# Wider V matmuls and one chunk of K in each of three units moved from DVE to PE in a two-layer decode kernel

## Chip, cores and metric

The kernel runs on one core of one Trainium2 chip. The metric is device time in microseconds (us) of one execution. The engines are named as the profile names them: PE (TensorE matmuls; PEld are its weight loads), DVE (VectorE), ACT (ScalarE), SP (SyncE, which issues the loads here). "Clock" is the share of full clock that the chip grants the PE array; the records show only 0.5 and 1.0 (129 periods of each in the trace before), and means of the two.

## What is computed

Two layers, each an attention block and a small MLP, for two batch entries and one query token. Cut to what matters:

```python
B, Sq, D = 2, 1, 576
H, Sk, Dh = 32, 16384, 128

def _A_ref(x, k_cache, v_cache, wq, wo):          # attention over a cache
    q = (x @ wq).reshape(B, Sq, H, Dh).transpose(0, 2, 1, 3)
    scores = einsum("bhqd,bhkd->bhqk", q, k_cache) * (Dh ** -0.5)
    p = softmax(scores)
    o = einsum("bhqk,bhkd->bhqd", p, v_cache)
    return o.transpose(0, 2, 1, 3).reshape(B, Sq, H * Dh) @ wo
# x = x + A(layernorm(x)); x = x + MLP(layernorm(x)); and both once more, with the same caches
```

There are 64 "units" (batch entry times head) per layer. One unit reads 4.19 MB of K and 4.19 MB of V, in bf16. Both layers together read 1096 MB, and each element of K and V that is read meets one multiplication per layer: this is a kernel of loads.

## The kernel before

SBUF has three places for a unit's K and V. Loads are queued as soon as the place is free; one layer keeps two units for the next. K arrives with a position per row, so a score needs either a transpose on PE, a copy out of PSUM on ACT and a matmul with one column (`turn`, `score`), or a multiplication and a sum on DVE (`dots`). A unit's 128 K blocks are 16 chunks of 8; `ncp` says how many chunks go to PE and ACT, the rest goes to DVE.

```python
def ncp(self, l, i):                              # chunks of unit i on PE; NCH is 16
    return self.NCH // 2 + (3, 2)[min(i, 1)] if l == 1 and i < 2 else self.NCH // 2 + 1

def turn(self, l, i, c):
    ...                                           # 8 transposes of 128x128 per chunk
            ins = pe.transpose(self.tps[b][:, j * 128:(j + 1) * 128],
                               kt[:, (j0 + j) * 128:(j0 + j + 1) * 128], self.ident[:, :])
    ...                                           # then ACT copies tps to ktsb
def score(self):
    ...                                           # 8 matmuls of ONE column
            ins = pe.matmul(self.sps[sp][:, col:col + 1], lhsT=self.ktsb[k][:, j, :],
                            rhs=self.qcur[:, sp:sp + 1], start=True, stop=True)
def weigh(self, l, i, h):                         # V work: 64 matmuls of ONE column per half
    ...
            ins = pe.matmul(self.ops[q][:, 0:1], lhsT=vt[:, j * 128:(j + 1) * 128],
                            rhs=self.p[q][:, h * self.TB + j:h * self.TB + j + 1], ...)
    ...
def attention(self, l):
    ...
    first = (2, self.ROT)[l]                      # ROT = 8: where the hardware loop starts
    self.s.loops.append((l * U + first, (U - first) // 2, 2, ...))
    for i in range(U):
        early = l == 1 and 1 <= i < first
        ...                                       # turn, score, dots of unit i, interleaved
                if early and c == 4:
                    self.weigh(l, i - 1, 0); self.weigh(l, i - 1, 1)
        ...
        if now: self.weigh(l, i - 1, 0)           # otherwise V work comes at the unit's END
        while self.waiting: self.score()
        if now: self.weigh(l, i - 1, 1)
```

Most units run in a hardware loop, two units to a turn, but units 0 and 1 of layer 1, units 0 to 7 of layer 2 and all of the MLPs are written out as straight-line code. And V work is the last PE work of a looped unit, while in the early units of layer 2 it sits in the middle, before the remaining transposes.

## Time and profile before

| | before |
|---|---|
| time, median of 3 runs | 2564.07 us (2563.78 to 2564.38) |
| bytes, mean rate | 1096.38 MB, 428 GB/s |
| load queue, share of 16 DMA engines | 99.7% |
| PE, DVE, ACT busy | 65%, 68%, 48% |
| mean granted PE clock | 0.674 |

The page of the profiled execution. The first line is the busy time of the engines; the next two have 40 columns, one per slice of 64 us (granted clock in tenths; GB/s). Then come the load queue (packets, MB, share of the 16 DMA engines' time), the chain that ended last by engine, and two of the costliest groups, PE's transposes and its V matmuls (busy us, mean ns of one, idle time just before and who ended it).

```profile
PE 1671.5 (65%) x36847; PEld 1559.0 (61%) x36847; DVE 1751.6 (68%) x2595; ACT 1231.3 (48%) x1944; POOL 1.0 (0%) x12
...
PEclk8666666666666666766666666666666666666665
...
GB/s 409 430 431 433 431 430 433 432 431 432 430 433 432 431 432 431 433 431 431 426 408 431 428 432 430 432 433 431 432 432 430 432 431 431 433 432 431 430 433 341
...
q1 hardware_dynamic: 46888, 1095.66, 99.7%
...
DMA 59%; issue 16%; DVE 13%; PE 10%; ACT 1%; SPq 0%; DVEq 0%
...
L798 PE MATMUL tps<-ident,buf 128*128 128x128 bf16 x9240 | 911.7, 263 | 616.5 <-DMA buf<-in_A_k_cache_dram 600.4
...
L870 PE MATMUL ops<-p,buf 128*128 128x1 bf16 x16384 | 461.7, 164 | 66.5 <-DMA buf<-in_A_v_cache_dram 57.4
```

The load queue is busy for 99.7% of the span, and the rate leaves 430 to 433 GB/s in only five slices: the first (409), three around the turn between the layers (426, 408, 428), and the last (341). The PE group of the transposes waited 600 us for K in all. PE's idle time is not the problem; it is the sign that something else sets the pace.

The same core in stretches: start and end, length, busy time of PE, PEld, DVE, ACT and POOL with counts, granted clock, DMA share, GB/s.

```profile
1180.00:1200.00 20.00, 12.69 (x282) 11.60 (x282) 13.74 (x21) 10.01 (x16) 0.00 (x0) 0.67 1.00 433
1280.00:1300.00 20.00, 13.68 (x285) 12.70 (x285) 3.05 (x19) 1.49 (x6) 0.00 (x0) 0.50 1.01 405
1300.00:1320.00 20.00, 16.35 (x323) 15.38 (x321) 7.85 (x19) 6.86 (x11) 0.00 (x0) 0.56 0.95 386
...
1340.00:1360.00 20.00, 16.75 (x341) 15.80 (x337) 16.35 (x26) 13.43 (x23) 0.00 (x0) 0.66 0.98 421
...
1380.00:1400.00 20.00, 18.01 (x355) 17.70 (x353) 18.15 (x27) 13.96 (x20) 0.00 (x0) 0.59 1.00 425
...
2550.00:2560.00 10.00, 9.74 (x143) 8.82 (x144) 0.17 (x1) 0.00 (x0) 0.00 (x0) 0.50 0.17 65
```

One ordinary stretch (1180), then the turn between the layers (1280, 1300), where transfer is lost; the stretches after it move 421 and 425 GB/s again. After about 2554 us there is nothing left to load.

PE's timeline at the end of a looped unit (start, length, operation, count; in brackets the idle time before it and what ended it), then in the third unit of layer 2:

```profile
654.22 0.61 PE L798 MATMUL tps<-ident,buf 128*128 128x128 bf16 x8
...
655.67 1.76 PE L870 MATMUL ops<-p,buf 128*128 128x1 bf16 x64 [0.40 <-DMA buf<-in_A_v_cache_dram]
...
657.69 1.78 PE L870 MATMUL ops<-p,buf 128*128 128x1 bf16 x64
...
666.81 0.50 PE L798 MATMUL tps<-ident,buf 128*128 128x128 bf16 x3 [7.21 <-DMA buf<-in_A_k_cache_dram]
```

```profile
1343.95 3.51 PE L870 MATMUL ops<-p,buf 128*128 128x1 bf16 x128 [0.26 <-ACT p L856]
1347.33 0.91 PE L798 MATMUL tps<-ident,buf 128*128 128x128 bf16 x7
1350.26 0.27 PE L798 MATMUL tps<-ident,buf 128*128 128x128 bf16 x1 [2.02 <-issue]
...
1350.58 1.01 PE L798 MATMUL tps<-ident,buf 128*128 128x128 bf16 x8
```

In the looped unit, transposes take 0.61 us per 8 (full clock), then V work (lines with `ops`) runs 64 matmuls in about 1.8 us, and then PE waits 7.2 us for the next K. In the early unit V work sits before transposes, and after it these take 1.01 us per 8 (half clock).

### The profile page before, as it was taken

What the parts mean: (1) busy time and instruction counts of PE and PEld (TensorE: products, weight loads), DVE (VectorE), ACT (ScalarE), POOL (GpSimd) and SP (SyncE); (2) the same over time, 40 slices, a digit from 0 to 9 for tenths busy, and PEclk for the clock granted to TensorE, in tenths of its full rate; (3) what the DMA queues carried; (4) which work ended last, traced back from release to release, by engine and by line L of the source; (5) the groups of instructions that cost most, each with busy time, mean ns of one, the idle gap of its engine ahead of it and who ended that gap; (6) DMA issues with size and microseconds to landing.
All of it is one profiled execution on the core that took longest, in us unless ns stands there. A gap on an engine that the chain in (4) does not pass through costs nothing.

```text
span 2562.7 us, 84020 instructions
## 1 busy us (share of the span) xinstructions
PE 1671.5 (65%) x36847; PEld 1559.0 (61%) x36847; DVE 1751.6 (68%) x2595; ACT 1231.3 (48%) x1944; POOL 1.0 (0%) x12
## 2 busy tenths in 40 slices
PE   5666666666666656666688766666656666665666
PEld 5555665565565656655678765565656555565566
DVE  5676767677666766766648777666767766676674
ACT  4544544454445445544446554454445544544452
POOL 0000000000000000000000000000000000000000
PEclk8666666666666666766666666666666666666665
DMA  9999999999999999999999999999999999999998
GB/s 409 430 431 433 431 430 433 432 431 432 430 433 432 431 432 431 433 431 431 426 408 431 428 432 430 432 433 431 432 432 430 432 431 431 433 432 431 430 433 341
DMA packets 46936, 1096.38 MB, mean 428 GB/s; under 512 B 4964, under 2 KB 6056, under 8 KB 11560
## 3 DMA queue, kind: packets, MB, share of 16 engines
q1 hardware_dynamic: 46888, 1095.66, 99.7%
q8 instruction: 40, 0.66, 0.1%
q14 instruction: 8, 0.07, 0.0%
HBM read 1095.64 MB, written 0.00 MB: 428 GB/s over the span
## 4 chain that ended last, share of the span: by engine, by line
DMA 59%; issue 16%; DVE 13%; PE 10%; ACT 1%; SPq 0%; DVEq 0%
DMA buf<-in_A_k_cache_dram 56%; DVE prod L827 11%; PE tps L798 6%; DMA buf<-in_B_w_dram 1%; DVE sd L830 1%; PE misc L846 1%; DMA buf<-in_A_v_cache_dram 1%; PE ops L870 1%; ACT ktsb L802 1%; PE misc L693 1%; DMA buf<-in_A_wq_dram 0%; PE sps L815 0%; SPq L435 0%; PE sps L655 0%; ACT p L856 0%
## 5 line engine op out<-in xcount | busy, mean ns | idle before, releaser
L802 ACT ACTIVATE ktsb<-tps 128x1024 bf16<-128x1024 bf16 x1155 | 1124.2, 1031 | 871.2 <-PE tps L798 866.2
L798 PE MATMUL tps<-ident,buf 128*128 128x128 bf16 x9240 | 911.7, 263 | 616.5 <-DMA buf<-in_A_k_cache_dram 600.4
L798 PEld LDWEIGHTS tps<-ident,buf 128*128 128x128 bf16 x9240 | 735.0, 120 | 643.1 <-DMA buf<-in_A_k_cache_dram 619.7
L830 DVE TENSOR_REDUCE sd<-prod 128x8 f32<-128x1024 bf16 x893 | 1089.5, 1220 | 31.0
L827 DVE TENSOR_TENSOR prod<-buf,qb 128x1024 bf16<-128x1024 bf16 x893 | 608.6, 682 | 11.4 <-DMA buf<-in_A_k_cache_dram 10.5
L870 PE MATMUL ops<-p,buf 128*128 128x1 bf16 x16384 | 461.7, 164 | 66.5 <-DMA buf<-in_A_v_cache_dram 57.4
L870 PEld LDWEIGHTS ops<-p,buf 128*128 128x128 bf16 x16384 | 443.7, 100 | 76.4 <-DMA buf<-in_A_v_cache_dram 66.4
L848 DVE TENSOR_REDUCE small<-misc 128x1 f32<-128x128 f32 x128 | 37.3, 292 | 635.8 <-PE misc L846 635.8
L815 PE MATMUL sps<-qcur,ktsb 128*128 128x1 bf16 x9240 | 396.8, 166 | 109.0 <-ACT ktsb L802 88.2
L815 PEld LDWEIGHTS sps<-qcur,ktsb 128*128 128x128 bf16 x9240 | 348.4, 101 | 172.2 <-ACT ktsb L802 166.1
L781 ACT ACTIVATE qb<-misc 128x128 bf16<-128x128 f32 x130 | 36.0, 277 | 369.2 <-PE misc L778 369.2
L846 PE MATMUL misc<-identS,small 128*128 128x128 f32 x256 | 94.4, 472 | 5.2 <-DVE small L840 5.2
L846 PEld LDWEIGHTS misc<-identS,small 128*128 128x128 f32 x256 | 69.7, 332 | 5.8 <-DVE small L840 5.7
L856 ACT ACTIVATE p<-sps,small 128x72 bf16<-128x72 f32 x128 | 41.4, 324 | 6.8 <-DVE small L848 6.8
L856 ACT ACTIVATE p<-sd,small 128x56 bf16<-128x56 f32 x128 | 44.6, 349 | 0.0
L773 ACT ACTIVATE qcur<-qt 128x1 bf16 (+1 forms) x130 | 29.4, 226 | 16.8 <-DVE qt L703 16.8
L778 PE MATMUL misc<-ident,qcur 128*128 128x128 bf16 x130 | 34.6, 266 | 1.3 <-ACT qcur L773 1.3
L925 PE MATMUL misc<-lpiece,small 128*128 128x16 f32 x28 | 8.5, 385 | 41.0 <-DVE lpiece L923 41.0
L925 PEld LDWEIGHTS misc<-lpiece,small 128*128 128x128 f32 x28 | 7.0, 311 | 43.6 <-DVE lpiece L923 43.6
L836 DVE TENSOR_REDUCE small<-sps 128x1 f32<-128x72 f32 x128 | 28.5, 223 | 4.1 <-PE sps L815 4.1
L693 PE MATMUL misc<-prod,buf 128*128 128x2 bf16 (+1 forms) x360 | 24.6, 179 | 6.6 <-DMA buf<-in_B_w_dram 4.6
L693 PEld LDWEIGHTS misc<-prod,buf 128*128 128x128 bf16 (+1 forms) x360 | 22.4, 111 | 8.8 <-issue 4.7
(94 smaller groups left out, 270.8 us busy)
## 6 DMA issues: line engine op xcount, KB each, us to landing
buf<-in_A_k_cache_dram SPq DMA_DIRECT2D x124, 4096.0 KB, 24.3
buf<-in_A_v_cache_dram SPq DMA_DIRECT2D x122, 4096.0 KB, 33.6
buf<-in_A_v_cache_dram SPq DMA_DIRECT2D x5, 2048.0 KB, 22.5
buf<-in_B_w_dram SPq DMA_DIRECT2D x8, 1152.0 KB, 30.7
buf<-in_A_wq_dram SPq DMA_DIRECT2D x8, 1024.0 KB, 9.0
buf<-in_A_wo_dram SPq DMA_DIRECT2D x14, 576.0 KB, 34.6
buf<-in_A_k_cache_dram SPq DMA_DIRECT2D x3, 2048.0 KB, 11.2
buf<-in_A_v_cache_dram SPq DMA_DIRECT2D x4, 1024.0 KB, 23.8
```

Of the source, the lines that this page charges most:

```text
L693: ins = pe.matmul(out[lo:128, t * self.B:(t + 1) * self.B], lhsT=w[:, t * 128:(t + 1) * 128 - lo], rhs=rhs, start=(first and t == 0), stop ...
L778: self.pe(lambda pe: pe.matmul(self.misc[:, 0:128], lhsT=bcast(self.qcur[:, q:q + 1], 128), rhs=self.ident[:, :], start=True, stop=True), ...
L781: self.act(lambda a: a.activation(out=self.qb[q][:, :], in_=self.misc[:, 0:128], func=ACT.Copy), r=["P:misc"], w=[f"qb{q}"])
L798: ins = pe.transpose(self.tps[b][:, j * 128:(j + 1) * 128], kt[:, (j0 + j) * 128:(j0 + j + 1) * 128], self.ident[:, :])
L802: self.act(lambda a: a.activation(out=self.ktsb[k][:, :, :].rearrange("p a b -> p (a b)"), in_=self.tps[b][:, :], func=ACT.Copy), r=[f"P:t ...
L815: ins = pe.matmul(self.sps[sp][:, col:col + 1], lhsT=self.ktsb[k][:, j, :], rhs=self.qcur[:, sp:sp + 1], start=True, stop=True)
L827: self.dve(lambda v: v.tensor_tensor(out=self.prod[d][:, :, :], in0=k3, in1=bcast_mid(self.qb[q][:, :], self.CH), op=ALU.mult), r=[*res, f ...
L830: self.dve(lambda v: v.tensor_reduce(out=self.sd[q][:, o:o + self.CH], in_=self.prod[d][:, :, :], axis=AX.X, op=ALU.add), r=[f"prod{d}"], ...
L846: self.pe(lambda pe: pe.matmul(self.misc[:, 128:256], lhsT=bcast(self.m[:, q:q + 1], 128), rhs=self.identS[:, :], start=True, stop=True), ...
L848: self.dve(lambda v: v.tensor_reduce(out=self.bias[:, q:q + 1], in_=self.misc[:, 128:256], axis=AX.X, op=ALU.max, negate=True), r=["P:misc ...
L856: self.act(lambda a, u, c0=c0, c1=c1, src=src: a.activation(out=self.p[q][:, c0:c1], in_=src, func=ACT.Exp, bias=self.bias[:, q:q + 1], sc ...
L870: ins = pe.matmul(self.ops[q][:, 0:1], lhsT=vt[:, j * 128:(j + 1) * 128], rhs=self.p[q][:, h * self.TB + j:h * self.TB + j + 1], start=(h ...
```

## The change

The intent rests on what the trace before shows: the clock falls while PE does its one-column V work (by the clock records, in 48 of the 49 looped units of layer 1 whose V work lies in 250-1220 us it is 1.0 when the V work begins and 0.5 when it ends). That this is because one column keeps the array busy for too little of the time was my guess; no run had shown it. With 32 equal columns per V matmul (only column 0 is used) the array should be busy for longer, the clock should stay full if the guess is right, and PE should then have room for a tenth chunk in the units early in layer 2, where units run back to back.

```diff
+    WIDE = 32
...
-        return self.NCH // 2 + (3, 2)[min(i, 1)] if l == 1 and i < 2 else self.NCH // 2 + 1
+        return self.NCH // 2 + ((3, 2, 2, 2, 2)[i] if l == 1 and i < 5 else 1)
...
-                    ins = pe.matmul(self.ops[q][:, 0:1], lhsT=vt[:, j * 128:(j + 1) * 128],
-                                    rhs=self.p[q][:, h * self.TB + j:h * self.TB + j + 1],
+                    at = h * self.TB + j
+                    ins = pe.matmul(self.ops[q][:, 0:self.WIDE], lhsT=vt[:, j * 128:(j + 1) * 128],
+                                    rhs=bcast(self.p[q][:, at:at + 1], self.WIDE),
                                     start=(h == 0 and j == 0), stop=(h == 1 and j == self.TB - 1))
```

Unit 1 of layer 2 had 10 chunks before; only units 2, 3 and 4 get one more on PE and one less on DVE.

## The prediction

> **What bounds it now.** The transfers. The queue table gives the one load queue 99.7% of the span on 16 DMA engines: 1096 MB at a mean of 428 GB/s, 430 to 433 in most slices. [...] A unit (8.39 MB of K and V) takes about 19.4 us of transfer, with PE busy 13 us, DVE 14, ACT 10 (table of stretches). In the chain of waits K loads hold 56%; PE waits 600 us in all for K, about 5.8 us per unit.
>
> Transfer time is lost at the start, in the turn between layers (405 GB/s in 1280-1300 us, 386 in 1300-1320), and at the end (no load after about 2554 us, while 180 matmuls of w4 run 12.3 us).
>
> **What the change does.** No load changes.
> 1. V work: 16384 matmuls of one column get 32. They now come every 27.5 ns (64 in 1.75 to 1.85 us) at either clock. In the timeline the clock falls with this work: transposes before it take 0.61 us per 8, after it 1.01. [...] Transposes of 128 columns come every 56 ns at full clock and 107 at half, so 32 columns should stream in 14 and 27 ns (estimate). I expect 27 to 31 ns per V matmul still, and full clock through it.
> 2. Layer 2, units 2 to 4: PE and ACT take 10 chunks, not 9 (unit 1 has 10 already), DVE 6, not 7. A chunk is 1.85 us on DVE, 1.03 on ACT.
>
> **What is on the path.** In a normal unit [...]the first 16 transposes stay at half clock (1.89 us); DVE's seven chunks (13 us) still set the compute. Saved PE time becomes waiting.
> Early in layer 2 (1325 to 1415 us) units run back to back in 14 to 16 us. I expect 12.5 to 13.5, until data is missing. But 1320 to 1480 us already moves 430 GB/s and K loads take up to 35 us from issue to landing, so the queue is full; at most 1 us can be won.
> The loss in the turn comes from w3, gelu, w4, layer norm and wq. Its w4 matmuls take 67 to 68 ns each, as did 25 like them at 37 us at a higher clock; neither turn nor end gains.
>
> **Prediction.** 2563 us, within 2557 to 2569. Faster by 2%: 0.01; within 2%: 0.98; slower: 0.01.
>
> **What would show it.** Span within 0.2%; DMA over 99%, same MB. Mean granted clock up from 0.674 to about 0.80. V matmuls 64 in 1.7 to 2.0 us. PE busy down from 1671 to 1550-1650 us, waits for K up. Layer 2's units 1 to 4 each 1.5 to 3 us shorter, then longer K waits before 1415 us. About 12.3 us of w4 matmuls at the end.
>
> **What would make it wrong.** If 32 columns do not overlap the weight load at half clock, V matmuls cost about 53 ns, 3.3 us more per unit: inside the 5.8 us of slack, but turn and end could lose 1 to 3 us each. If the queue does run dry early in layer 2 (at 1333 us a V load came only just in time), earlier frees win 1 to 3 us.

Its sum stays 2563 us: the span before, less at most 1 us that loads could still win. That loads are near their limit rests on the 99.7% of the queue and the 430 to 433 GB/s of most slices alone, and "full clock through it" was a guess. The trace before has the transposes 55 ns (median) from start to start at full clock and 107 at half, V matmuls 25 and 27, and the clock at 0.76 during the 25 matmuls at 37 us, for 0.50 during those of the end. That weight loads and matmuls overlap shows in PE and PEld busy for 65% and 61% of one span; the 53 ns without overlap are an estimate, 27 ns between V matmuls and 27 of streaming, both at half clock, one after the other.

## The result

The changed kernel took 2563.49 us (median of 4 runs, 2563.30 to 2563.77), the kernel before 2563.93 us in the runs beside it. The ratio is 0.9998, with a 95% interval of 0.9981 to 1.0016: no difference. Ratios here and below are the mean time of one kernel's fast runs over that of the other's in the same rounds, so not quite the ratio of the medians quoted.

The page after, with the lines that answer those of before (the queue's line is the same to the digit, the chain has DMA at 60% for 59%):

```profile
PE 1659.3 (65%) x36895; PEld 1545.7 (60%) x36895; DVE 1746.4 (68%) x2589; ACT 1232.8 (48%) x1947; POOL 1.0 (0%) x12
...
PEclk8767777677667766767768777777677767777676
...
GB/s 409 430 430 433 431 431 433 431 430 433 430 433 431 431 433 431 430 432 432 426 412 428 428 431 434 431 430 433 432 429 432 432 432 431 429 434 432 430 431 347
...
L799 PE MATMUL tps<-ident,buf 128*128 128x128 bf16 x9264 | 902.4, 260 | 619.1 <-DMA buf<-in_A_k_cache_dram 600.4
...
L874 PE MATMUL ops<-p,buf 128*128 128x32 bf16 x16384 | 463.5, 181 | 68.6 <-DMA buf<-in_A_v_cache_dram 58.2
```

The clock row rose here and there (mean 0.674 to 0.723) and nothing else moved: same bytes, same rate slice by slice, same 600.4 us of waiting for K. PE busy fell by only 12 us, far less than I expected. The stretches after the turn:

```profile
1280.00:1300.00 20.00, 13.50 (x288) 12.42 (x288) 3.06 (x19) 1.49 (x6) 0.00 (x0) 0.50 1.02 409
1300.00:1320.00 20.00, 16.26 (x323) 15.14 (x324) 7.99 (x19) 7.00 (x11) 0.00 (x0) 0.58 0.95 384
...
1380.00:1400.00 20.00, 15.00 (x383) 14.41 (x383) 14.90 (x23) 12.60 (x19) 0.00 (x0) 0.91 1.00 428
```

The transfer rates are those of before within a few GB/s, though PE's clock is much higher in the 1380 stretch (0.91 for 0.59). The timelines, first of the same looped unit, then of the third unit of layer 2:

```profile
655.61 1.77 PE L874 MATMUL ops<-p,buf 128*128 128x32 bf16 x64 [0.39 <-DMA buf<-in_A_v_cache_dram]
...
657.62 1.84 PE L874 MATMUL ops<-p,buf 128*128 128x32 bf16 x64
...
666.75 0.50 PE L799 MATMUL tps<-ident,buf 128*128 128x128 bf16 x3 [7.18 <-DMA buf<-in_A_k_cache_dram]
```

```profile
1345.23 3.37 PE L874 MATMUL ops<-p,buf 128*128 128x32 bf16 x128
1348.45 0.55 PE L799 MATMUL tps<-ident,buf 128*128 128x128 bf16 x7
1351.41 0.27 PE L799 MATMUL tps<-ident,buf 128*128 128x128 bf16 x1 [2.42 <-issue]
...
1351.73 1.01 PE L799 MATMUL tps<-ident,buf 128*128 128x128 bf16 x8
```

V work costs what it did: 64 matmuls in 1.77 and 1.84 us, for 1.76 and 1.78. In the looped unit nothing follows it except 7.2 us of waiting, so even a clock held through it would have nothing to speed up. In the early unit it works as intended for 7 transposes (0.55 us for 7, where before they took 0.91), and then an idle time without releaser comes (2.42 us), after which the clock is at half again. These idle times early in layer 2, totals from 1280 to 1500 us, before and then after (us in total, times, longest):

```profile
PE ops L870 <- issue: 4.1, 3, 1.7
...
PE tps L798 <- issue: 2.9, 3, 2.0
...
PE sps L815 <- issue: 1.5, 2, 0.9
```

```profile
PE ops L874 <- issue: 6.8, 4, 2.7
PE sps L816 <- issue: 6.2, 3, 2.4
...
PE tps L799 <- issue: 5.3, 3, 2.4
```

With one gap of 1.8 us in the MLP, the same in both and not shown, that is 4.1 + 2.9 + 1.5 + 1.8 = 10.3 us before, and 6.8 + 6.2 + 5.3 + 1.8 = 20.1 us after. From query matmul to query matmul, units 1 to 4 of layer 2 took 15.0, 15.4, 15.7 and 14.2 us before, and 15.6, 17.2, 15.8 and 15.9 us after. They became longer, not shorter, and the total did not notice.

Taken together, PE spent the 60.3 us of these four units before with 51.3 us of work, 4.8 us of idle time without releaser and 3.9 us of waiting for ACT; after, the 64.4 us were 52.7, 8.5 and 3.0 (the rest are short gaps; worked out from the traces). So PE's work did not shrink: three moved chunks bring 24 transposes and 24 score matmuls, which took what the higher clock gave. Most of the added length is idle time without releaser. These are single executions, though: `tail_pieces` and `unroll24` below, whose code is the same here, showed 16.8 and 10.9 us of such idle time in 1280-1500 us, for 20.1, and took 61.9 and 62.6 us for the four units.

### The profile page after: what moved, and what is told of

Its sections match the earlier page's. It is cut to its first block, busy times and chain, and to the rows that moved or that the text cites. A ratio compares the mean times of both kernels' runs of the same rounds, so it can differ in the third digit from the quotient of the medians.

```text
span 2561.6 us, 84113 instructions
## 1 busy us (share of the span) xinstructions
PE 1659.3 (65%) x36895; PEld 1545.7 (60%) x36895; DVE 1746.4 (68%) x2589; ACT 1232.8 (48%) x1947; POOL 1.0 (0%) x12
## 3 DMA queue, kind: packets, MB, share of 16 engines
q1 hardware_dynamic: 46888, 1095.66, 99.7%
## 4 chain that ended last, share of the span: by engine, by line
DMA 60%; issue 16%; DVE 13%; PE 10%; ACT 1%; SPq 0%; DVEq 0%
DMA buf<-in_A_k_cache_dram 53%; DVE prod L828 11%; PE tps L799 5%; DMA buf<-in_A_v_cache_dram 4%; DMA buf<-in_B_w_dram 3%; DVE sd L831 1%; PE misc L847 1%; PE ops L874 1%; PE misc L694 1%; ACT ktsb L803 1%; PE sps L816 0%; DMA buf<-in_A_wq_dram 0%; SPq L436 0%; DVE small L849 0%; SPq L421 0%
## 5 line engine op out<-in xcount | busy, mean ns | idle before, releaser
L799 PE MATMUL tps<-ident,buf 128*128 128x128 bf16 x9264 | 902.4, 260 | 619.1 <-DMA buf<-in_A_k_cache_dram 600.4
L799 PEld LDWEIGHTS tps<-ident,buf 128*128 128x128 bf16 x9264 | 727.0, 119 | 643.2 <-DMA buf<-in_A_k_cache_dram 617.5
L831 DVE TENSOR_REDUCE sd<-prod 128x8 f32<-128x1024 bf16 x890 | 1085.8, 1220 | 30.8
L874 PE MATMUL ops<-p,buf 128*128 128x32 bf16 x16384 | 463.5, 181 | 68.6 <-DMA buf<-in_A_v_cache_dram 58.2
L857 ACT ACTIVATE p<-sps,small 128x72 bf16<-128x72 f32 (+1 forms) x128 | 41.7, 326 | 6.3 <-DVE small L849 6.3
L857 ACT ACTIVATE p<-sd,small 128x56 bf16<-128x56 f32 (+1 forms) x128 | 44.7, 349 | 0.0
L774 ACT ACTIVATE qcur<-qt 128x1 bf16 (+1 forms) x130 | 29.6, 228 | 16.9 <-DVE qt L704 16.9
L837 DVE TENSOR_REDUCE small<-sps 128x1 f32<-128x72 f32 (+1 forms) x128 | 28.5, 223 | 11.9 <-PE sps L816 11.9
```

The lines of the kernel that those rows point to most:

```text
L799: ins = pe.transpose(self.tps[b][:, j * 128:(j + 1) * 128], kt[:, (j0 + j) * 128:(j0 + j + 1) * 128], self.ident[:, :])
L831: self.dve(lambda v: v.tensor_reduce(out=self.sd[q][:, o:o + self.CH], in_=self.prod[d][:, :, :], axis=AX.X, op=ALU.add), r=[f"prod{d}"], ...
L857: self.act(lambda a, u, c0=c0, c1=c1, src=src: a.activation(out=self.p[q][:, c0:c1], in_=src, func=ACT.Exp, bias=self.bias[:, q:q + 1], sc ...
L874: ins = pe.matmul(self.ops[q][:, 0:self.WIDE], lhsT=vt[:, j * 128:(j + 1) * 128], rhs=bcast(self.p[q][:, at:at + 1], self.WIDE), start=(h ...
```

## The experiments

Four theories. **T**: transfers bind everywhere that counts, so nothing done to PE, ACT or DVE shows. **C**, a rival: the two halves of the change cancel. **G/H**: 32 columns are too few to hold the clock (H), and a held clock would have won time (G). **F**: PE waits for its own instructions wherever code is not looped, which explains the early units. All 12 experiments gave a result; the edits are against the changed kernel unless told otherwise.

### The halves alone

`wide_alone` puts the old `ncp` back; `chunks_alone` has `WIDE = 1`.

> V work 32 columns wide, chunks as before. Theory T (the transfers bind, so nothing on PE, ACT or DVE counts): within 0.15% of before, DMA share over 99%. Rival C (the two parts cancel: the wider V work gains, the moved chunks lose, or the other way round): this run and the run with the chunks alone differ from before by over 0.3% in opposite directions. Profile: granted clock as in the changed kernel, about 0.72.

> 10 chunks on PE in units 1 to 4 of layer 2, V work one column wide. Theory T: within 0.15% of before. Rival C: over 0.3% away, opposite in sign to the run with the wide V work alone. Profile: granted clock as before, about 0.675; units 2 to 4 of layer 2 not shorter than before if PE waits for its instructions there.

Measured: 2563.88 us with the wide V work alone (ratio 0.9998, interval 0.9982 to 1.0015, clock 0.727), 2563.45 us with the chunks alone (0.9999, 0.9982 to 1.0015, clock 0.675). Neither half does anything, so C falls. Both halves act where they should: the first moves the clock, the second does not. With the chunks alone units 2 to 4 took 15.6, 15.6 and 16.0 us, so they are not shorter either; there the idle time without releaser was as before (10.7 us in 1280-1500 us), and it is PE's work that grew, to 53.4 us in units 1 to 4.

### More columns

```diff
-    WIDE = 32
+    WIDE = 64      # wide64;  WIDE = 128 in wide128
```

> As the changed kernel, but 64 columns. At full clock a V matmul comes every 27.5 ns; 32 columns are about 14 ns of array time, half of it, 64 are 27 ns, nearly all of it (estimate from the 56 ns of 128 columns). Theory H (32 columns keep the array busy enough only at half clock): the clock now stays full through the V work, mean granted clock 0.78 to 0.85 instead of 0.72. [...] Time: theory T within 0.15% of before either way; rival G (the gain is missing because the clock was not held) over 0.5% faster than before.

> As the changed kernel, but 128 columns: about 56 ns per V matmul at full clock, so 3.6 us more PE work per unit, about 460 us in all. Theory T: PE has 5.8 us idle per unit, so within 0.3% of before, PE busy up to about 2050 to 2200 us, PE's waits for K down by 350 to 450 us. Rival E (PE's work is on the path): 5 to 18% slower. Clock at or above that of 64 columns.

With 64 columns: 2564.18 us (ratio 1.0003, interval 0.9986 to 1.0019), clock 0.834. That is in the range of H. The clock records, laid over the matmuls of units 10 to 59 of layer 1, show it directly: the share of V matmuls that began at full clock was 0.54 before, 0.56 with 32 columns and 0.89 with 64; of the transposes it was 0.49, 0.54 and 0.54. So in this kernel 32 columns did not hold the clock through V work and 64 mostly did, and the transposes gained nothing by it. That 32 are too few wherever they stand does not follow: in `light_after` below they bring the V matmuls from 0.71 to 1.00. What decides it there, no run isolates. G falls: the clock was the one wanted and nothing was won. The V work of one looped unit in that run:

```profile
911.56 3.46 PE L874 MATMUL ops<-p,buf 128*128 128x64 bf16 x64 [0.71 <-DMA buf<-in_A_v_cache_dram]
...
915.28 2.14 PE L874 MATMUL ops<-p,buf 128*128 128x64 bf16 x64
```

The second half shows what 64 columns cost at full clock, 2.14 us, so 33 ns each and not the 27.5 I had written; the first half began at half clock and took 3.46, 54 ns each.

With 128 columns the clock is 0.907, a V matmul takes 68 ns in the mean over both clocks (1113.7 us over 16384; the 56 expected were a guess from the transposes, for full clock), the transposes take 226 ns each instead of 260 in the mean, PE is busy 2153.9 us, and PE's waits for K fall from 600.4 to 60.7 us. The time is 2578.87 us, ratio 1.0063 (1.0046 to 1.0080). About 500 us of added PE work cost 15 us. The looped units still take the same: 19.61 us in the mean of units 10 to 59 of layer 1, for 19.64 before. So the slack was real: 600.4 us in 105 waits, 5.7 us each, or 4.7 us per unit over all 128. The waits fell by 540 us, more than the 350 to 450 I had expected, and the 15 us are more than the 0.3% that I had allowed T. In stretches:

```profile
1240.00:1260.00 20.00, 17.04 (x287) 15.46 (x285) 14.12 (x21) 9.89 (x17) 0.00 (x0) 0.91 1.00 429
...
1280.00:1300.00 20.00, 12.93 (x285) 12.06 (x284) 3.73 (x23) 1.49 (x6) 0.00 (x0) 0.68 0.77 288
...
1340.00:1360.00 20.00, 18.35 (x327) 17.68 (x325) 12.54 (x18) 10.46 (x16) 0.00 (x0) 0.91 0.88 366
```

An ordinary stretch (1240) moves 429 GB/s with PE busy 17 of 20 us. The loss is in the turn: DMA share 0.77 and 288 GB/s in 1280-1300 us, where before it was 1.01 and 405, and 0.88 in 1340-1360. Counted by bytes delivered, this trace and the one before are level within 0.5 us up to 550 MB and 12 us apart at 700 MB, so most of the loss is there. In the chain that ended last V work has 26%, for 1% before: it is likely on the path to the frees that the next loads wait for, a reading of the trace that no run isolates. So T needs its limit said: nothing shows as long as loads are queued; in the turn, PE can take the queue dry.

### Loads made light

If transfers hide the change, it should show without them. In these kernels an eighth of V is loaded in nearly all units and used eight times. Their outputs are wrong, which doesn't matter for the times. (The comparison with the reference passed them all the same, so the differences must lie within its tolerance.)

```diff
-                ring.want([(kind, l, u, h) for h in range(2)], at, unit, [lambda e, v: e.dma_start(v, ap)],
+                m = unit // 8 if kind == "V" else unit
+                ring.want([(kind, l, u, h) for h in range(2)], at, unit,
+                          [lambda e, v: e.dma_start(v[:, 0:m], ap[:, 0:m])],
...                                                                   # and in weigh:
-                    lhsT=vt[:, j * 128:(j + 1) * 128]
+                    lhsT=vt[:, (j % 16 if light else j) * 128:][:, 0:128]   # vt: half 0's buffer
```

`light_before` is the kernel before with this, `light_after` the changed one. `light_ten1`, `light_ten32` and `light_ten64` have, besides, 10 chunks on PE in all units (11 in the first of layer 2, as ever) and 1, 32 and 64 columns.

> The kernel before, but of V only an eighth is loaded in nearly all units, and used eight times (wrong result on purpose; all compute instructions as before). Bytes per unit 4.72 MB instead of 8.39, 10.9 us at 432 GB/s (estimate). Theory T: the unit falls from 19.4 us to what DVE needs, seven chunks of 1.85 us and about 1.3 us of small work, 14 to 15 us: time 1900 to 2060 us, DMA share 75 to 85%. Rival E (the engines bind already): time falls by under 5%.

> The changed kernel with the same light loads (wrong result on purpose). With the transfers out of the way DVE's seven chunks should bind, which a faster PE does not shorten: within 2% of the light kernel before, perhaps 0.5 to 2% faster because the first transposes and the maximum matmuls of a unit, which DVE waits for, run at full clock. If the clock is worth much as soon as transfers do not bind: over 4% faster.

> Light loads, 10 of 16 chunks on PE and ACT in all units, V work one column wide (wrong result on purpose). DVE then needs 12.4 us per unit, ACT 12, PE 12 to 14 depending on the clock. Expected 1750 to 1950 us, faster than the light kernel before, PE the bound where its clock falls. Units 1 to 7 of layer 2, whose instructions are not looped, longer than looped units by 1.5 to 3 us if PE waits at every second block of its instructions there.

> The same with V work 32 columns wide. If the clock is what PE-bound units lack: 3 to 8% faster than the one-column version of it, granted clock above 0.8. If not: within 1.5%. Units 1 to 7 of layer 2 again longer than looped ones.

> Light loads, 10 chunks everywhere, 64 columns. The clock is fuller than with 32 (above 0.92), but a V matmul issued at half clock costs 53 ns instead of 27.5. Expected within 1.5% of the 32-column version (1877 us): if clock share alone counted, 1 to 2% faster.

| kernel | time us | ratio to before | clock | median unit us (10 to 59, layer 1) |
|---|---|---|---|---|
| before | 2564.30 | 1 | 0.674 | 19.4 |
| light_before | 2077.06 | 0.8098 | 0.676 | 14.7 |
| light_after | 2059.68 | 0.8031 | 0.839 | 14.8 |
| light_ten1 | 1968.73 | 0.7681 | 0.774 | 13.8 |
| light_ten32 | 1877.25 | 0.7320 | 0.909 | 13.1 |
| light_ten64 | 1962.90 | 0.7659 | 0.950 | 13.8 |

(The last ran on another chip than the four above it; the ratios to before, taken on the same chip each, are comparable.)

Compute unchanged, fewer bytes: 19% faster, just above the top of my range. T holds, and the rival that the engines bind already falls. The load queue and the chain of the first light kernel, then the chain of `light_ten1`:

```profile
q1 hardware_dynamic: 46888, 647.92, 77.0%
...
issue 44%; DVE 33%; PE 16%; DMA 3%; ACT 2%; DVEq 1%; SPq 0%; ACTq 0%
```

```profile
PE 54%; ACT 23%; issue 16%; DMA 3%; DVE 2%; ACTq 1%; DVEq 0%; SPq 0%
```

In the first, DVE leads the chain besides "issue", and DMA has 3%; in the second PE has 54%. That DVE sets the pace of the first shows in the step to `light_ten1`, which takes one chunk per unit off DVE and is 5.2% faster, at 1968.73 us; that is just above the 1750 to 1950 us that I had expected. With DVE binding, the change brings 2077.06 to 2059.68 us, 0.8%, as expected. With PE binding, 32 columns bring 1968.73 to 1877.25 us: 4.6%. So the gain that the change was built on exists (the clock goes from 0.774 to 0.909), and it pays where PE binds. It does not pay in the real kernel. Units 1 to 7 of layer 2 took 14.2 to 16.9 us in `light_ten1` and 14.0 to 16.6 us in `light_ten32`, 1.6 and 1.9 us more in the mean than the median looped unit; 0.7 and 1.3 us of it were idle time without releaser.

The 64 columns were a miss: 4.6% slower than 32 columns (0.7659 over 0.7320), where I expected within 1.5%. The clock was nearly full anyhow, and a V matmul costs 33.4 ns for 27.5 (64 in 2.14 us, for 1.75): 128 of them are 0.75 us more per unit, times 128 units 97 us (an estimate from the timelines above), against the 86 us measured. (The 53 ns in that expectation are an estimate too, half of the 107 ns between transposes of 128 columns at half clock; the 64 V matmuls of `wide64` that began there took 54 ns each.)

### Straight-line code

F first rests on what the traces show. The instruction queue of the trace moves packets of 16,384 bytes. In the kernel before, none of them falls between 95 and 1278 us, where layer 1 is looped; from 1278 us on, while the MLP and the first units of layer 2 run, one comes every 6 to 9 us. In the changed kernel I counted the PE records (matmuls, weight loads and the few of its sequencer) from one idle time without releaser to the next:

```
idle time ends at (us)           1336.9 1351.4 1366.5 1380.0 1387.0 1400.8 1415.1 1429.6
PE records since the one before     -     511    513    512    256    512    512    512
16 KB instruction packet near it 1334.3 1349.1 1364.1 1377.4 1384.4 1398.4 1412.6 1427.1
```

From the packet at 1334.3 us to the one at 1427.1 us there are 13 steps from packet to packet, and PE went through 3328 records between the first and the last of these idle times, 13 times 256: one packet for 256 records, or 64 bytes each. So I read a packet as the next 256 of PE's instructions and the idle time as a wait for it; the trace names no releaser. The waits were 1.4 to 2.4 us in most of these cases. How much shows differs between the runs: in 1280-1500 us the kernel before had such gaps of 0.2 to 2.0 us, `wide128`, where PE takes longer for the same instructions and fetches as many packets, none at all. Why mostly every second block shows, stays open. To test that straight-line code is the cause, 24 units of layer 1 were written out, in the light kernel and in the changed one:

```diff
-        first = (2, self.ROT)[l]
+        first = (26, self.ROT)[l]
```

> The light kernel with 10 chunks everywhere and 32 columns, but units 2 to 25 of layer 1 are written out instead of looped: the same work by the same instructions in the same order. Theory F (code that is not looped makes PE wait for blocks of 256 of its instructions; seen so far as idle time of 1.4 to 2.7 us with no releaser, every 256 or 512 PE records, beside instruction packets of 16 KB): the instruction queue grows from 41 packets to 90 to 105, the same gaps appear in units 2 to 25, these units take 14 to 16 us instead of 13.0, time 1900 to 1940 us against 1877. Rival (the first units of layer 2 are long for their own order of work or late loads): units 2 to 25 stay at 13.0 us, time within 0.5%.

> The changed kernel with full loads, units 2 to 25 of layer 1 written out. Theories T and F together: gaps of 1 to 2.7 us appear in PE in these units, 14 or so us of PE waiting per 6 units, and the time stays within 0.2% of before, since PE has 5.8 us to spare per unit; instruction bytes rise by under 1 MB of 1096. Rival (PE gaps reach the total): 1% or more slower.

Light: 1890.65 us (1882.78 to 1893.36), ratio to before 0.7363, against 0.7320 looped; 97 instruction packets for 41. The median of units 5 to 24 rose from 13.00 to 14.01 us, and that of the units after them, looped in both, stayed at 13.12. F holds for the unit. The total rose by 13 us (11 by the ratios; the two ran on different chips) and not by 23 or more: the mean unit rose by only 0.67 us (13.58 to 14.25), since units with a piece of the output projection absorbed it.

Full loads: I expected within 0.2%, and it took 2574.60 us, ratio 1.0041 (1.0025 to 1.0056). A miss. The queues of that run, and PE's waits in 100-530 us:

```profile
q1 hardware_dynamic: 46888, 1095.66, 99.4%
q8 instruction: 92, 1.51, 0.2%
```

```profile
PE tps L799 <- DMA buf<-in_A_k_cache_dram: 102.0, 19, 7.3
PE ops L874 <- issue: 15.2, 8, 2.8
```

The gaps appear (15.2 us in V work, 0.8 in scores), though far fewer than the 14 us per 6 units that I had expected, and PE's waits for K shrink from 110.8 us in the changed kernel to 102.0. So the gaps were paid out of slack, as T has it, and they can't be the 10.7 us. Something slowed the loads: in 100-530 us they ran at 427 GB/s, for 432 in the changed kernel. Bytes don't explain it: 0.85 MB more is 2 us at 428 GB/s. But each load's completion is counted 16 times (the 246 loads of 4 MB of K and V have 3936 counts in the trace before), as many times as there are DMA engines, and the trace has the times of these counts. I take each for one engine's share of the load; the trace names no engine. The time from the first to the last count of one load, as a median over loads that landed in a window (worked out from the completion records):

```
loads landing in (us)   60-160  160-260  260-360  360-520  520-700  900-1240  1340-1400  1500-2400
before                    3.4     3.4      3.4      3.4      3.5      3.6       3.1        6.2
changed kernel            3.4     3.4      3.4      3.4      3.4      3.5       2.1        5.2
unroll24                  3.3     4.9      8.0      9.6     11.8     10.7       3.2        6.2
```

While instruction packets flow, the spread grows, from 3.3 to 11.8 us; when the loop starts at 520 us, it stops growing, and it lasts until the turn. If each count is one engine's, one or more of the 16 fall behind the others, by 8 us. PE goes on only after the last count (in the kernel before its transposes start 46 ns after it, the median of 44 waits for K in 250-1220 us), so each K comes later by what the last engine lost: unit 26 of layer 1 began at 532.9 us, for 523.3 us in the changed kernel. Which engines carry the instruction packets the trace does not say, so "they carry the packets and fall behind for that" is the likely reading, not a shown one. A like step appears in the kernels before and after, from 2 or 3 us at 1340-1400 us to 5 or 6 us past the early units of layer 2. In two traces where the loads pause it did not pile up: in `wide128` it rises from 1.6 to 3.4 us there and drops to 1.7 us after a stretch at 347 GB/s (1460-1480 us), and in `light_unroll24`, with 97 instruction packets, it stays near 2 us.

### A stretch where nothing hides

As a counterpart, an edit of the end, where PE has the core to itself:

```diff
-    W4_PIECES = ((1, 2, 3, 3, 2, 1), (5, 4, 2, 1))
+    W4_PIECES = ((1, 2, 3, 3, 2, 1), (3, 3, 3, 2, 1))
```

> The changed kernel, with the w4 loads of layer 2 cut into pieces of 3, 3, 3, 2, 1 groups instead of 5, 4, 2, 1, so that the first piece lands about 2 us sooner (864 KB less at about 430 GB/s) and the 180 matmuls of w4 at the very end (12.3 us, after a wait for that piece) start sooner. This is a stretch without other loads to hide behind. Theory T: time down by 1.5 to 2.5 us, which the total shows although it did not show any of the PE work saved elsewhere; the profile's last w4 matmuls start about 2 us earlier relative to the end of the gelu. Otherwise: no change.

The timeline of the end of the changed kernel (the w4 matmuls, the sum after them), then of this one:

```profile
2546.22 12.35 PE L694 MATMUL misc<-prod,buf 128*128 128x2 bf16 x180 [4.61 <-DMA buf<-in_B_w_dram]
2558.61 0.17 DVE L741 TENSOR_TENSOR xn<-xsum,misc 128x10 bf16<-128x10 f32 x1 [15.04 <-PE misc L694]
```

```profile
2543.89 6.22 PE L694 MATMUL misc<-prod,buf 128*128 128x2 bf16 x90 [2.50 <-DMA buf<-in_B_w_dram]
...
2551.09 6.18 PE L694 MATMUL misc<-prod,buf 128*128 128x2 bf16 x90 [0.97 <-DMA buf<-in_B_w_dram]
2557.31 0.17 DVE L741 TENSOR_TENSOR xn<-xsum,misc 128x10 bf16<-128x10 f32 x1 [13.96 <-PE misc L694]
```

The matmuls start 2.3 us sooner (2543.89 for 2546.22), but pause once for a load (0.97 us), so the sum comes 1.3 us sooner. Time: 2562.30 us (2562.16 to 2562.74, 5 runs), for 2563.93 of the kernel before on the same chip (2563.56 to 2564.86, 9 runs). The runs don't overlap, but the interval of the ratio (0.9993, 0.9980 to 1.0007) includes 1, so it is a small gain (1.6 us, at the low end of the 1.5 to 2.5 expected) that fits the profile rather than a proven one. It was not timed beside the changed kernel.

## Why the prediction was right, and where it was not

The time was right: 2563 predicted, 2563.49 measured, and for the reason given. Point by point:

- *Transfers bind, PE has about 5.8 us of slack per unit.* Right, with 4.7 us as the mean over all units. Fewer bytes made the kernel 19% faster with all compute in place; 3.9 us more of PE work per unit (494.6 us in `wide128`) left the looped units at 19.6 us.
- *V matmuls stay at 27 to 31 ns.* Right: 463.5 us busy for 461.7, 64 in 1.75 to 1.9 us (from start to start 25 ns at full clock and 27 at half, before and after).
- *Neither the end nor the turn gains.* Right: 180 w4 matmuls of 12.35 us after, 12.29 before; 409 and 384 GB/s in the turn for 405 and 386.
- *"Mean granted clock up from 0.674 to about 0.80."* Wrong: 0.723. The failed step was "full clock through it": the clock was full when the V work of those 49 looped units began, and it fell to half by the end of it in 32 of them (48 before). My own estimate had 32 columns in 14 of 27.5 ns at full clock, half of the time; 64 columns gave 0.834, 128 gave 0.907. The clock periods in the traces before and after last whole multiples of 3.41 us (the last, cut-off one of each apart). That the clock follows the share of the time in which the array streams would fit the four means (0.674, 0.723, 0.834 and 0.907 for 1, 32, 64 and 128 columns), but `light_after`, where 32 columns kept nearly every looped V matmul at full clock (0.99 to 1.00), says that width alone does not decide it; the rule stays open.
- *"PE busy down from 1671 to 1550-1650 us, waits for K up."* Wrong: 1659 us, and 600.4 us of waits in both. V work is the last PE work of a looped unit, and where the clock held through it (17 of the 49 units) it was lost again before K came: the first 16 transposes after each of the 44 waits of over 2 us for K in 250-1220 us ran at half clock, before and after alike. Even at clock 0.834 the transposes took 260 ns in the mean, as at 0.723.
- *"Layer 2's units 1 to 4 each 1.5 to 3 us shorter."* Wrong: 0.1 to 1.8 us longer. My 12.5 to 13.5 us per unit is about PE's work alone, which measured 13.2 us in the mean after the change (12.8 before). The sum left out PE's waits for blocks of instructions, 8.5 us in these four units and 20.1 us in 1280-1500 us, which the timeline before showed as idle time without releaser (10.3 us), and 3.0 us of waiting for ACT. That these waits come with straight-line code is shown (`light_unroll24`: 13.00 to 14.01 us per unit); their size changes from execution to execution (10.9 to 20.1 us with the same code), so how much of the growth is due to the change stays open.
- *"Turn and end could lose 1 to 3 us each" with slower V matmuls.* Not tested as it stands, at 53 ns (an estimate, see above); at 68 ns per V matmul (1113.7 us over 16384) the total lost 15 us, most of it in the turn. With 64 columns, 54 ns only at half clock, it lost nothing that shows (2564.18 us).

The total was safe from the three wrong steps because each concerned time that PE has to spare. That also means that the total alone would have passed them all.

## What to carry to other kernels

Before costing an engine's savings, ask which wait ends last in that stage: here it is that for K: the 494.6 us of PE work that 128 columns added came almost wholly out of PE's waiting, and only the stretches without queued loads (the turn, the end) could show one. A wider matmul that kept the clock up was worth something here only where PE bound and more PE work followed it before the next long wait: 4.6% in the kernel with light loads and ten chunks, nothing in this one. Idle time without a releaser came in the early units of layer 2 of the changed kernel after every 256 or 512 PE records, beside instruction packets of 16 KB; look for such a pattern in straight-line code before planning to fill that engine, and remember that the loads, too, ran slower here while such fetches were under way (427 for 432 GB/s).
